# One written-out instruction order, two moves: a block of scores ahead of two transposes, and one weight load behind a softmax product

## The chip, the cores and the metric

The kernel runs on one core of a Trainium2 chip (trn2). A core has five engines with instruction queues of their own: TensorE (PE in the profile, its weight loads PEld), VectorE (DVE), ScalarE (ACT), GpSimd (POOL) and SyncE (SP), and 16 DMA engines that they share. Each queue runs in order. The metric is the time of one execution on the device in microseconds, as a median of several runs. A profiled execution gives, beside its own time, a trace of every instruction, every DMA packet and the TensorE clock that was granted.

## What the kernel computes

A causal attention with a window of 64 positions, whose output goes straight into a two-layer block with a cosine gate:

```python
scores = q @ k.transpose(0, 1, 3, 2) / np.sqrt(D)     # q, k, v: 8 batches, 8 heads, 576 positions, 64
rel = pos[:, None] - pos[None, :]
scores = np.where((rel >= 0) & (rel < 64), scores, -1e9)
scores = scores - np.max(scores, axis=-1, keepdims=True)
attn = np.exp(scores)
attn = attn / (np.sum(attn, axis=-1, keepdims=True) + 1e-09)
x = (attn @ v).transpose(0, 2, 1, 3).reshape(4608, 512)
h = x @ w_in                                          # w_in: 512 x 2048
out = (h * np.cos(h)) @ w_out                         # w_out: 2048 x 512
```

Inputs and output are float32; the matmuls take bf16.

## The kernel before

**Tiling.** The 4608 rows of x are cut into nine token tiles of 512. For each, TensorE multiplies by w_in (the columns of 128 give 16 results, h), ScalarE makes the sine with a phase of pi/2, VectorE multiplies h by it, and TensorE multiplies by w_out. The attention of a later batch is worked into the matmuls of an earlier tile. Only the beginning has nothing to hide behind: tile 0 needs the attention of batch 0 first, and that is what this case is about.

**The order at the beginning** is written out by hand in the string `FIRST` (lines 52 to 71). A loop (line 724) splits it into steps and calls one function for each; since every engine's queue is in order, the order of the string is the order on each engine. A later planner (`at`, `pump`, lines 615 to 622) orders the rest and isn't touched. The steps that matter here, with the pair of heads as first number and, for scores, a half of the query blocks (0 or 1) as the second:

- `Lq0`, `Lk0`, `Lq1`, `Lk1`, `Lv0`: loads of q, k (L169) and v (L192), issued from GpSimd, which casts on the way. (The first pair of batch 0, `Lq0.0` and `Lk0.0`, comes through SyncE instead, L174.) `Lwi.i` loads a quarter of w_in (L208), `Lwo.i` a quarter of w_out (L211). Each is an instruction on GpSimd's queue of 0.6 to 0.9 us.
- `tq`, `tk` (batch 0) and `Tq`, `Tk` (batch 1): twelve transposes on TensorE of one pair of heads into PSUM (L225), in a ring of three buffers. `pq`, `pk`, `Pq`, `Pk` copy the result to SBUF, on VectorE (`.d`) or ScalarE (`.a`) (L130, L259, L261).
- `s.p.g.bank`: the scores of one group of batch 0, that is four blocks of 64 queries of a pair of heads, into a PSUM bank (L358 puts the mask into the bank with two matmuls, L365 adds eight score matmuls). `Gs` is the same for batch 1.
- `m`: the negative maximum of a group (VectorE, L375). `e`: the exponentials and their sums (ScalarE, L392). `i`: the reciprocal of the sums (VectorE, L402). `n.p.g.p`: the product of the two, `w`, on GpSimd (L409). `w.p.g`: four transposes of it on TensorE (L425). `c`: its copy to SBUF (VectorE, L130).
- `zA`, `zB`, `zC`: copies of half a v block to other partitions. `v.a.g`: the products with v (L462), `x.a.g`: their copy to xT (ScalarE or VectorE, L130).
- `h.g.f.bank`: a half of tile 0 times two column blocks of w_in (L476), eight matmuls. `h.0.0` and `h.0.1` read the first piece of w_in, `h.0.2` and `h.0.3` the second, `h.0.4` and `h.0.5` the third, `h.0.6` and `h.0.7` the fourth.

`s.p.g` frees nothing until its exponentials are done: the five banks are shared by the groups, and a bank can be written again after `e` has read it (for `s.3.0` the bank of group `0.0`, for `s.2.1` that of group `0.1`).

In the span of the change the order on TensorE is `s.2.0`, `Tq.0`, `Tk.0`, `s.3.0`, `Tq.1`, `Tk.1`, `s.2.1`, `Gs.10`, `Gs.9`, `w.0.0`, `w.1.0`, `Gs.12`, `w.2.0`, `w.3.0`, `v.0.0`, and on GpSimd `Lv0.3`, `Lwi.0`, `Lwi.1`, `Lwi.2`, `n.1.0`, `n.0.0`, `n.2.0`, `n.3.0`, `n.0.1`, `n.1.1`, `n.2.1`, `Lwi.3`. Four transposes of a constant (L423) stand in front of those of `w.3.0`.

Of the kernel before, what the change touches and what calls it, by code (L numbers as in the profile page):

```python
# [10 lines left out]
def _safe_warn(msg, *a, **kw):  # L11
# [40 lines left out]
FIRST = (  # L52
    "io Lq0.0 Lk0.0 mk cq.d mc ck.a tq.0 fa.1 Lq0.1 pq.0.d Lk0.1 tk.0 fb.1 pk.0.a s.0.0.0 Lq0.2 tq.1 fc.1 tk.1 m.0.0 "
    "pq.1.a s.0.1.1 Lk0.2 tq.2 pk.1.d s.1.0.2 Lq0.3 Lk0.3 tk.2 s.1.1.3 e.0.0 tq.3 m.0.1 Lq1.0 Lk1.0 Lq1.1 pq.2.d "
    "pk.2.d Lk1.1 tk.3 m.1.0 s.2.0.4 Lv0.0 Lv0.1 Tq.0 Lv0.2 pk.3.d m.2.0 e.0.1 pq.3.a i.0.0 e.1.0 Tk.0 s.3.0.0 Tq.1 "
    "e.2.0 Lv0.3 Lwi.0 Pq.0.d i.1.0 Lwi.1 m.3.0 m.1.1 i.2.0 Pk.0.a e.3.0 Lwi.2 Tk.1 n.1.0.p s.2.1.1 Pq.1.d Gs.10.2 "
    "m.2.1 Gs.9.4 n.0.0.p Pk.1.a n.2.0.p i.3.0 e.1.1 w.0.0 zA.0.d w.1.0 c.0.0.d Gs.12.0 w.2.0 n.3.0.p i.0.1 c.1.0.d "
    "zA.1.d c.2.0.d e.2.1 zB.0.s zB.1.s n.0.1.p i.1.1 w.3.0 v.0.0 c.3.0.d x.0.0.a s.3.1.3 Gm.10 v.1.0 m.3.1 i.2.1 "
    "Gs.11.2 Gm.9 Gm.12 n.1.1.p x.1.0.a e.3.1 w.0.1 w.1.1 c.1.1.a i.3.1 h.0.0.1 h.0.1.4 tb n.2.1.p c.0.1.d Lwi.3 "
# [744 lines left out]
```

## Time and profile before

| what | us |
|---|---|
| time, median of three runs | 296.46 |
| the three runs | 296.46, 296.06, 297.11 |
| the profiled execution's own time | 297.33 |
| its span, first to last instruction | 295.5 |
| what lies around the span (297.33 less 295.5) | 1.8 |
| TensorE busy in the span | 288.2 |
| mean granted TensorE clock (1 is full) | 0.994 |

The span is what the engines' rows add up to, with times counted from its start. A row of the timeline has the start, the duration (of several merged instructions their total stretch), the engine, the line, the operation, what it writes and reads, and, in brackets, how long the engine was idle before it and what ended that. The chain of work that ended last has the start, the duration, the engine and the line. A row of the windows has, for a stretch of time, the busy time of each engine, the granted clock, the share of the DMA engines' time and GB/s; a DMA share above 1 means that packets overlapped in an engine. In a row of DMA issues the last number is the time from issue to landing.

### The profile page before, as it was taken

The page shows a single profiled execution, that of the slowest core. Times are in us where ns is not written, and L with a number is a line of the kernel's source. Part 1 is how long each engine was busy: PE and PEld are TensorE (multiplying, and loading weights), DVE is VectorE, ACT ScalarE, POOL GpSimd, SP SyncE. Part 2 cuts the span into 40 slices and gives each one's busy share as a digit, 9 for nine tenths or more (in the row PEclk, how much of TensorE's full clock was granted, in tenths as well). Part 3 has the DMA queues.
Part 4 walks back from the last instruction along what each step waited for, and adds up shares of the span by engine and source line. Part 5 has one row for each costly group of instructions (what it writes and reads, how often), then busy time and mean ns, then how long its engine had stood idle before and what let it go on. Part 6 is the DMA issues. An engine that isn't in the chain of part 4 may idle for free.

```text
span 295.5 us, 8290 instructions
## 1 busy us (share of the span) xinstructions
PE 288.2 (98%) x2815; PEld 163.4 (55%) x2815; DVE 231.0 (78%) x906; ACT 237.9 (80%) x791; POOL 209.9 (71%) x230
## 2 busy tenths in 40 slices
PE   8879999999999999999999999999999999999995
PEld 3658864544454444444454445444547854884495
DVE  3987888888797876788668876996689868957863
ACT  5989699887988799869986999699967896937710
POOL 9899749993699849995999399948995476033200
PEclk9989999999999999999999999999999999999999
DMA  7999999999999999999999999999959315042013
GB/s 145 177 198 190 186 196 137 151 129 153 151 265 128 151 235 172 114 182 215 174 166 150 225 172 152 155 213 179 146 129 194 41 38 177 2 114 86 0 38 107
DMA packets 168267, 43.81 MB, mean 148 GB/s; under 512 B 155616, under 2 KB 163872, under 8 KB 168224
## 3 DMA queue, kind: packets, MB, share of 16 engines
q0 software_dynamic: 100896, 18.06, 82.3%
q1 hardware_dynamic: 67184, 25.15, 47.0%
q8 instruction: 22, 0.36, 0.5%
q14 instruction: 21, 0.17, 0.2%
q10 hardware_dynamic: 144, 0.07, 0.1%
HBM read 36.70 MB, written 9.44 MB: 156 GB/s over the span
## 4 chain that ended last, share of the span: by engine, by line
PE 93%; POOL 3%; DVE 2%; issue 0%; ACT 0%; POOLq 0%
PE h_ps L512 37%; PE out_ps L764 24%; PE out_ps L601 13%; PE h_ps L476 5%; PE o_ps L444 3%; PE out_ps L495 3%; PE s_ps L327 3%; POOL w L409 2%; PE busy L137 2%; PE tw_ps L425 1%; DVE negm L375 1%; DVE kT L130 1%; PE o_ps L462 1%; PE s_ps L365 1%; POOL v L130 0%; PE tk_ps L225 0%
## 5 line engine op out<-in xcount | busy, mean ns | idle before, releaser
L512 PE MATMUL h_ps<-xT,w_in 128*128 128x512 bf16 x512 | 111.8, 379 | 0.0
L409 POOL TENSOR_TENSOR w<-e,rden 128x512 bf16<-128x512 f32 (+1 forms) x68 | 69.4, 1033 | 48.8 <-DVE rden L402 38.1
L751 DVE TENSOR_TENSOR gT<-h_ps,sin 128x512 bf16<-128x512 f32 x128 | 84.6, 687 | 21.8 <-ACT sin L748 20.4
L392 ACT ACTIVATE e<-s,negm 128x128 f32<-128x128 f32 (+1 forms) x256 | 97.2, 382 | 2.6 <-DVE negm L380 1.6
L748 ACT ACTIVATE sin<-h_ps 128x512 f32<-128x512 f32 x128 | 73.5, 599 | 25.3 <-PE h_ps L512 23.5
L512 PEld LDWEIGHTS <-w_in 128*128 128x128 bf16 x512 | 50.2, 98 | 59.3
L764 PE MATMUL out_ps<-w_out,gT 128*128 128x512 bf16 x320 | 72.0, 379 | 0.0
L380 DVE CUSTOM_DVE_ANT_0 s<-s_ps,mask 128x128 f32<-128x128 f32 (+1 forms) x256 | 55.7, 276 | 0.3 <-PE s_ps L327 0.3
L764 PEld LDWEIGHTS <-gT 128*128 128x128 bf16 x320 | 30.4, 98 | 35.5
L392 ACT ACTIVATION_READ_ACCUMULATOR e<-s,negm 128x1 f32 x256 | 48.1, 188 | 0.0
L192 POOL DMA_DIRECT2D v<-in_v_dram x40 | 34.0, 869 | 0.7 <-DMA q<-in_q_dram 0.5
L186 POOL DMA_DIRECT2D q<-in_q_dram x30 | 26.2, 892 | 3.3 <-PE tq_ps L225 3.0
L186 POOL DMA_DIRECT2D k<-in_k_dram x30 | 26.2, 884 | 0.0
L402 DVE RECIPROCAL rden<-den 128x4 f32<-128x4 f32 (+1 forms) x73 | 12.0, 166 | 18.0 <-ACT e L392 17.8
L130 POOL COPY v<-v 64x1536 bf16<-64x1536 bf16 (+3 forms) x16 | 22.9, 1431 | 0.4
L380 DVE DVE_READ_ACCUMULATOR2_ANT negm<- 128x1 f32 x256 | 21.2, 83 | 0.0
L541 POOL TENSOR_TENSOR qT<-gT 128x512 bf16<-128x512 bf16 x12 | 13.6, 1156 | 9.1 <-DVE gT L751 9.0
L130 DVE CAST xT<-o_ps 128x512 bf16<-128x512 f32 x24 | 15.5, 681 | 5.1 <-PE o_ps L444 4.5
L601 PEld LDWEIGHTS <-gT 128*128 128x128 bf16 x152 | 13.9, 98 | 2.2
L495 PE MATMUL out_ps<-w_out,gT 128*128 128x512 bf16 x64 | 14.7, 380 | 0.0
L476 PE MATMUL h_ps<-xT,w_in 128*128 128x256 bf16 x128 | 14.6, 273 | 0.0
L572 DVE TENSOR_TENSOR out_sb<-out_ps,p 128x512 f32<-128x512 f32 (+2 forms) x16 | 8.6, 548 | 6.7 <-ACT p L130 5.6
(92 smaller groups left out, 327.9 us busy)
## 6 DMA issues: line engine op xcount, KB each, us to landing
out_dram<-out_sb SPq DMA_DIRECT2D x16, 512.0 KB, 8.4
v<-in_v_dram POOLq DMA_DIRECT2D x32, 128.0 KB, 5.9
q<-in_q_dram POOLq DMA_DIRECT2D x24, 128.0 KB, 8.6
k<-in_k_dram POOLq DMA_DIRECT2D x24, 128.0 KB, 6.5
w_in<-in_moe_w_in_dram POOLq DMA_DIRECT2D x4, 512.0 KB, 9.2
w_out<-in_moe_w_out_dram POOLq DMA_DIRECT2D x4, 512.0 KB, 10.9
q<-in_q_dram POOLq DMA_DIRECT2D x7, 144.0 KB, 6.2
k<-in_k_dram POOLq DMA_DIRECT2D x7, 144.0 KB, 6.3
```

The lines of the kernel that those rows point to most:

```text
L130: {"a": nc.scalar.copy, "p": nc.gpsimd.tensor_copy}.get(engine, nc.vector.tensor_copy)(out, in_)
L186: nc.gpsimd.dma_start(out=st[name, b][0:n, c].rearrange("p (h d) -> p h d", h=H), in_=src.rearrange("h p d -> p h d"))
L192: nc.gpsimd.dma_start(out=vt.rearrange("p (h d) -> p h d", h=H), in_=v[b, :, c * 128:c * 128 + n, :].rearrange("h p d -> p h d"))
L380: nc.vector.tensor_tensor_reduce(out=s[:, u, c], in0=s_ps[:, u, c], in1=mask[:, 2 - j % 2 if j else 0, c], scale=-scale if b else -1.0, sc ...
L392: nc.scalar.activation(e[:, u, c], s[:, u, c], AF.Exp, bias=negm[:, u:u + 1], scale=1.0 if n < n_first else -1.0, accum_out=den[:, u:u + 1])
L409: (nc.gpsimd if engine == "p" else nc.vector).tensor_tensor(out=w[:, 0:u], in0=e[:, 0:u], op=ALU.mult, in1=rden[:, 0:u].unsqueeze(2).to_br ...
L476: nc.tensor.matmul(out=h_ps[:, half * e:half * e + half], lhsT=w_in_sb[:, ks, ff * 128:ff * 128 + 128], rhs=st["xT", 0][:, ks, half * g:ha ...
L512: nc.tensor.matmul(out=st["h", ff], lhsT=w_in_sb[:, ks, ff * 128:ff * 128 + 128], rhs=st["xT", mt][:, ks], start=start, stop=stop)
L601: nc.tensor.matmul(out=to[n_] if split else to[:, e], lhsT=lhs[name][f // 2][:, f % 2, 128 * e:128 * e + 128], rhs=rhs[name][:, f, lo:hi], ...
L748: nc.scalar.activation(sin, h_ps, AF.Sin, bias=math.pi / 2.0)
L751: nc.vector.tensor_tensor(out=gt[:, e], in0=h_ps, in1=sin, op=ALU.mult)
L764: nc.tensor.matmul(out=o_ps[e], lhsT=gT[ff // 2][:, ff % 2, ms * 128:ms * 128 + 128], rhs=w_out_sb[:, ff], start=ff == 0, stop=ff == n_ff - 1)
```

## The change

Two moves in `FIRST`, and nothing else:

- TensorE: `s.3.0` goes ahead of `Tk.0`, and `s.2.1`, which stood behind `Tk.1`, goes with it. The order is then `s.2.0`, `Tq.0`, `s.3.0`, `s.2.1`, `Tk.0`, `Tq.1`, `Tk.1`, `Gs.10`. The banks stay as they were.
- GpSimd: `Lwi.2` goes from ahead of `n.1.0` to behind it. The order is then `Lwi.1`, `n.1.0`, `Lwi.2`, `n.0.0`.

No instruction is added or removed, and the orders on VectorE and ScalarE are the same as before.

```diff
-    "pk.2.d Lk1.1 tk.3 m.1.0 s.2.0.4 Lv0.0 Lv0.1 Tq.0 Lv0.2 pk.3.d m.2.0 e.0.1 pq.3.a i.0.0 e.1.0 Tk.0 s.3.0.0 Tq.1 "
-    "e.2.0 Lv0.3 Lwi.0 Pq.0.d i.1.0 Lwi.1 m.3.0 m.1.1 i.2.0 Pk.0.a e.3.0 Lwi.2 Tk.1 n.1.0.p s.2.1.1 Pq.1.d Gs.10.2 "
+    "pk.2.d Lk1.1 tk.3 m.1.0 s.2.0.4 Lv0.0 Lv0.1 Tq.0 Lv0.2 pk.3.d m.2.0 e.0.1 pq.3.a i.0.0 e.1.0 s.3.0.0 s.2.1.1 "
+    "Tk.0 Tq.1 e.2.0 Lv0.3 Lwi.0 Pq.0.d i.1.0 Lwi.1 m.3.0 m.1.1 i.2.0 Pk.0.a e.3.0 Tk.1 n.1.0.p Lwi.2 Pq.1.d Gs.10.2 "
```

## The prediction, made before the changed kernel was run

> **What bounds the kernel now.** I read the page first, then the chain of waits in order of time, then the timelines of the engines over the stretch that the change touches, and last the landings of the loads.
>
> ```profile
> PE 93%; POOL 3%; DVE 2%; issue 0%; ACT 0%; POOLq 0%
> ```
>
> The chain that ended last is TensorE for 93% of the span. A change outside it must move the place where TensorE takes over. The chain in order of time shows that place:
>
> ```profile
> 13.27 0.64 DVE qT L130
> 13.91 0.08 DVE rden L402
> 13.99 0.59 DVE negm L375
> 14.65 0.74 POOL w_in L208
> 15.39 0.07 issue
> 15.45 4.10 POOL w L409 x4
> 19.60 0.56 PE tw_ps L425 x4
> 20.15 0.57 PE o_ps L462 x8
> ...
> 28.07 10.59 PE h_ps L476 x96
> ```
>
> From 14.65 to 19.60 GpSimd carries the chain: the issue of w_in's third piece, then four products w (`n.1.0`, `n.0.0`, `n.2.0`, `n.3.0`). At 19.60 TensorE gets the last of them (`w.3.0`) and from there the chain is its own work, but for a few later pieces on other engines that wait on that work in turn. So what makes the fourth product ready earlier moves the rest with it, as far as nothing else stands in the way.
>
> **The load behind the product.** GpSimd's timeline:
>
> ```profile
> 10.67 1.75 POOL L192 DMA_DIRECT2D v<-in_v_dram  x2 [0.47 <-DMA q<-in_q_dram]
> 12.40 1.51 POOL L208 DMA_DIRECT2D w_in<-in_moe_w_in_dram  x2
> 14.64 0.74 POOL L208 DMA_DIRECT2D w_in<-in_moe_w_in_dram  x1 [0.73 <-DVE negm L375]
> 15.45 6.13 POOL L409 TENSOR_TENSOR w<-e,rden 128x512 bf16<-128x512 f32 x6
> ```
>
> GpSimd is idle for 0.73 us (13.91 to 14.64), then issues for 0.74, and the first product starts at 15.45. That product needs its exponentials and one reciprocal, and the chain has the end of that reciprocal at 13.91 + 0.08 = 13.99. After the change it can start there. What does the issue wait for? The profile names VectorE's maximum, which a load into w_in does not use. A row above has another GpSimd load waiting for the landing of a q load: counted in the written order, the thirteenth load from GpSimd waits for the fifth, eight back. The third piece of w_in is the seventeenth, so its ninth is q of batch 1's pair 1:
>
> ```profile
> 6.92 0.68 POOL L169 DMA_DIRECT2D q<-in_q_dram  x1
> ```
>
> ```profile
> q<-in_q_dram POOLq DMA_DIRECT2D x1, 144.0 KB, 7.4
> ```
>
> ```profile
> 14.40 0.45 PE L225 MATMUL tq_ps<-ident,q 96*64 96x96 bf16 x12 [0.76 <-DMA q<-in_q_dram]
> ```
>
> That q landed about 7.4 us after its issue at 6.92, at 14.3, and TensorE's transposes of it began at 14.40 at its landing. I take this landing for the wait. Behind the product the issue comes at 15.0, when it is long past.
>
> The sum from 13.99: before, to the end of the fourth product, 15.45 + 4.10 = 19.55. After: one product (4.10 / 4 = 1.025) to 15.02, the issue (0.74) to 15.76, the gap (0.07), three products (3.08) to 18.91. Gain 0.64; its bounds are 0.58 with another such gap and 0.73, the whole idle time.
>
> The second and third products need reciprocals that are older than their turn, and the fourth one that comes at 16.83:
>
> ```profile
> 15.17 0.72 DVE L130 COPY qT<-tq_ps 128x576 bf16<-128x576 bf16 x1
> 15.81 0.68 DVE L375 TENSOR_REDUCE negm<-s_ps 128x4 f32<-128x512 f32 x1
> 16.83 0.18 DVE L402 RECIPROCAL rden<-den 128x4 f32<-128x4 f32 x1 [0.34 <-ACT e L392]
> 17.98 0.42 DVE L130 COPY wT<-tw_ps 128x512 bf16<-128x512 bf16 x1 [0.34 <-PE tw_ps L425]
> 18.83 0.85 DVE L130 COPY v<-v 64x512 bf16<-64x512 bf16 x1
> ```
>
> It ends at 17.01; the product's turn is 17.88. The copy of the first transposed w waits 0.34 for TensorE at 17.98, and with the second product 0.64 earlier that wait is gone; VectorE is then late next: its copy of v ends at 19.68 - 0.34 = 19.34, and TensorE wants it for `v.0.0` at 20.15 - 0.64 = 19.51. Cover 0.17.
>
> What the moved issue pushes: behind it stand only products, all earlier than before. The piece itself is issued at 15.02 instead of 14.64, 0.38 later. Its landing:
>
> ```profile
> w_in<-in_moe_w_in_dram POOLq DMA_DIRECT2D x1, 512.0 KB, 8.2
> w_in<-in_moe_w_in_dram POOLq DMA_DIRECT2D x1, 512.0 KB, 11.9
> w_in<-in_moe_w_in_dram POOLq DMA_DIRECT2D x1, 512.0 KB, 5.7
> ```
>
> ```profile
> 23.59 0.80 POOL L208 DMA_DIRECT2D w_in<-in_moe_w_in_dram  x1
> ```
>
> ```profile
> 28.00 3.23 PE L476 MATMUL h_ps<-xT,w_in 128*128 128x256 bf16 x28
> ```
>
> The landings are those of the first, third and fourth pieces, then stand the issue of the fourth and the matmuls that read the third and fourth. The third needs 11.9 us from issue to landing (14.64 + 11.9 = 26.5), the first 8.2 (12.40 + 8.2 = 20.6): 5.9 us between the two landings where the issues are 2.2 apart, so the third queues behind older loads and an issue 0.38 later should change its landing by nothing; the bound is 0.38. Its reader is `h.0.4` at 28.00, 27.36 after the gain: cover 0.4 to 0.8.
>
> [...] The two issues from 12.40 took 1.51, 0.76 each, with a bf16 copy beside them (13.27 in the chain), against 0.74 beside maxima; by the rows it is 0.02.
>
> **The scores ahead of the transposes.** TensorE's timeline, and ScalarE's copy of `Tk.0`:
>
> ```profile
> 13.04 0.40 PE L358 MATMUL s_ps<-mask,ident 64*64 64x512 bf16 x2
> 13.28 0.36 PE L365 MATMUL s_ps<-kT,qT 64*64 64x64 bf16 x8
> 14.70 0.45 PE L225 MATMUL tk_ps<-ident,k 96*64 96x96 bf16 x12
> 15.08 0.40 PE L358 MATMUL s_ps<-mask,ident 64*64 64x512 bf16 x2
> 15.32 0.75 PE L365 MATMUL s_ps<-kT,qT 64*64 64x128 bf16 x22
> 17.55 0.62 PE L425 MATMUL tw_ps<-ident,w 128*128 128x128 bf16 x8 [1.48 <-POOL w L409]
> ```
>
> ```profile
> 14.71 0.69 ACT L130 COPY kT<-tk_ps 128x576 bf16<-128x576 bf16 x1
> ```
>
> `s.2.1` (two mask matmuls, eight scores, 15.08 to about 15.5) moves into the hole of 0.76 that ends at 14.40. `s.3.0` moves from 13.04 to about 12.6. `Tk.0` then begins near 13.4 and ends near 13.8; ScalarE copies it at 14.71, so 0.9 us of cover. `Tq.1` stays at its landing, 14.40, and `Tk.1` at 14.70. Nobody takes the earlier scores up earlier: VectorE works without a pause until the maxima of `s.3.0` (13.99) and `s.2.1` (15.81). `Gs.10` needs ScalarE's copy that ends at 15.40. So this half is worth nothing on the path, and its loss is bounded by the cover. If `Tk.0` came over 0.9 us late, ScalarE would stall with all exponentials behind it.
>
> **The clock.** Three stretches of 3.41 us, each with its length, the busy times of PE, PEld, DVE, ACT and POOL, the granted clock, the DMA share and GB/s:
>
> ```profile
> 12.86:16.27 3.41, 2.45 (x70) 1.79 (x64) 3.41 (x9) 3.41 (x20) 2.62 (x4) 1.00 2.29 158
> 16.27:19.69 3.42, 1.77 (x25) 1.25 (x26) 2.71 (x7) 3.42 (x20) 3.42 (x5) 1.00 1.31 205
> 19.69:23.10 3.41, 3.41 (x58) 2.49 (x58) 2.89 (x18) 1.81 (x7) 2.39 (x3) 0.50 1.23 220
> ```
>
> After a stretch with 52% busy TensorE (1.77 of 3.42) the granted clock is 0.50 for the next, after one with 72% it stays 1.00. The half clock falls where TensorE has taken over, so it can cost up to 3.41 / 2 = 1.7 us. With the w chain 0.64 earlier, 1.77 becomes some 2.4 of 3.42 (70%), near the stretch that kept the clock. What would then be late is the third piece: landing 26.5, reader at 28.00, so at most 1.5 of gain in all. For the fourth (23.59 + 5.7 = 29.3, read 24 matmuls after 28.00 at 10.59 / 96 each, 30.65) the limit is 1.35, unless its earlier issue brings it forward.
>
> [...]
>
> **The sum.** Profiled execution, 297.33: 0.64 gives 296.7 with the half clock kept, the limit of 1.35 to 1.5 gives 295.8 to 296.0 without. But it is 0.87 above the median of 296.46 and above all three runs. The three lie 1.05 apart, about what half a clock costs after the landings have cut it, so I read the low one, 296.06, as an execution that does not pay it, and has little left to gain before the landings bind. The median run then gains something between 0.2 and 0.8. I take the chain's 0.64, trimmed to 0.6: 295.9, own range 295.5 to 296.4. About 0.3% (0.9 us) is what a measurement of this kernel can tell from no change, so this is inside it.
>
> **The rivals.**
>
> 1. The clock and the chain both pay in the median run. For it: 70% against the 72% that kept the clock. Against: the landings. 296.46 less 1.35 to 1.5 gives 295.0 to 295.1; faster by over 0.3%.
> 2. The 0.73 of idle time belongs to GpSimd and not to the load: whatever ended with VectorE's maximum holds the product too. It then starts at 14.65, the issue follows at 15.67, and the fourth product ends at 19.55 as before. For it: the profile names that maximum. Against: the landing at 14.3 and the 13th load's wait. Or the landings hide all. 296.3 to 296.5.
> 3. Slower: the early stretch is emptied. `s.2.1` leaves 15.08, and with the holes after 13.8 a stretch that begins at 13.6 holds 14.40 to 15.1 and a few scores, some 1.2 of 3.41 us, a third. The clock is then halved from 17.0, and what lies there (17.55 to 19.60) takes twice as long; if TensorE also fails to win it back for the next stretch, the whole takeover runs at half clock: 296.46 + 1.35 = 297.8. It decides when two halved stretches follow one another. Against: the stretch at 0.50 was busy throughout and the clock came back after it; with one halved stretch the gain of 0.64 is lost and little more.
>
> **How the numbers follow.** Forecast 0.55, first rival 0.23, second 0.15, third 0.07. Faster by over 0.3% (below 295.57): the first rival and a little of the forecast's range, 0.30. Slower: 0.07. Same: 0.63. The predicted time is 295.9. The range runs from the first rival's 295.0 to 296.8, the second's upper end and the spread of the runs above it.
>
> **What would show it.** Right: the first product on GpSimd at 14.0, the issue of w_in at 15.0 with no wait before it, the fourth product's end near 18.9, `w.3.0` near 18.95, `Tk.0` near 13.4 with ScalarE's copy still at 14.71, and the third piece landing at 26.5. The clock rows tell the first and third rivals: no 0.50 stretch between 19 and 23, or one that begins near 17. Wrong: a first product at 14.6; `h.0.4` or `h.0.6` waiting for w_in; ScalarE idle before 14.71; a span below 294 or above 296.5.

## The result, and the profile after

The change made the kernel 0.6% slower.

| | before | after |
|---|---|---|
| time, median of 19 runs each, us | 296.98 | 298.86 |
| lowest and highest, us | 295.55, 299.17 | 297.36, 300.56 |
| ratio after to before, 95% interval | | 1.0062 [1.0044, 1.0081] |
| the profiled execution's own time, us | 297.33 | 298.86 |
| its span, us | 295.5 | 297.1 |
| its mean granted TensorE clock | 0.994 | 0.989 |

The chain that ended last, by engine, after. TensorE's share was 93% before:

```profile
PE 89%; POOL 3%; DMA 2%; DVE 2%; issue 1%; ACT 1%; POOLq 0%
```

The same chain in order of time (start, duration, engine, line). GpSimd, which carried it from 14.65 to 19.60 before, does not occur in this stretch:

```profile
15.41 1.42 ACT e L392 x8
16.83 0.02 issue
16.86 0.18 DVE rden L402
17.04 2.29 DVE v L130
19.33 0.33 DVE wT L130
...
20.08 0.94 DVE v L130
21.02 0.04 issue
21.06 0.53 PE o_ps L462 x12
```

TensorE takes over at 21.06 instead of 19.60. One row stands out: VectorE spends 2.29 us of the chain on a copy of v, `zA.0`, which was no part of it before. GpSimd's timeline after shows that GpSimd itself did what was predicted:

```profile
14.31 1.04 POOL L409 TENSOR_TENSOR w<-e,rden 128x512 bf16<-128x512 f32 x1
15.30 0.81 POOL L208 DMA_DIRECT2D w_in<-in_moe_w_in_dram  x1
16.12 3.05 POOL L409 TENSOR_TENSOR w<-e,rden 128x512 bf16<-128x512 f32 x3
19.82 1.04 POOL L409 TENSOR_TENSOR w<-e,rden 128x512 bf16<-128x512 f32 x1 [0.65 <-DVE rden L402]
```

The issue stands behind the first product, waits for nothing, and the fourth product ends at 16.12 + 3.05 = 19.17 (before 19.55). Now VectorE's timeline after:

```profile
16.95 2.37 DVE L130 COPY v<-v 64x512 bf16<-64x512 bf16 x1
19.25 0.41 DVE L130 COPY wT<-tw_ps 128x512 bf16<-128x512 bf16 x1
19.67 0.38 DVE L130 COPY wT<-tw_ps 128x512 bf16<-128x512 bf16 x1
20.08 0.93 DVE L130 COPY v<-v 64x512 bf16<-64x512 bf16 x1
```

The copy of 64x512 began at 16.95, as before (16.93), but lasted 2.37 us instead of 0.72. (The same copy lasts 0.29 us in e6 below, so its row holds its wait; where such a row starts is called below where the copy "asks".) It ended at 19.32, 0.16 behind the end of the third of the three products (19.17). The copies of the transposed w behind it came at 19.25 and 19.67 instead of 17.98 and 18.41. TensorE's timeline after shows who waited for them:

```profile
17.24 0.62 PE L425 MATMUL tw_ps<-ident,w 128*128 128x128 bf16 x8 [1.22 <-POOL w L409]
19.71 0.59 PE L423 MATMUL tw_ps<-ident 128*128 128x128 bf16 x4 [0.55 <-DVE wT L130]
20.09 0.63 PE L425 MATMUL tw_ps<-ident,w 128*128 128x128 bf16 x4
24.43 2.04 PE L476 MATMUL h_ps<-xT,w_in 128*128 128x256 bf16 x16
29.22 1.49 PE L476 MATMUL h_ps<-xT,w_in 128*128 128x256 bf16 x12
```

The first transposes of w come earlier (17.24 for 17.55), so the load's move did what it was for. Then the ring of three transposed tiles is full until VectorE empties one: `w.3.0` starts at 20.09 instead of 19.60, `h.0.0` at 24.43 instead of 23.34, `h.0.4` at 29.22 instead of 28.00. Of the 1.6 us by which the span grew, 1.2 are there by then. The row of `h.0.0` before:

```profile
23.34 1.91 PE L476 MATMUL h_ps<-xT,w_in 128*128 128x256 bf16 x16
```

The stretches of the granted clock after (length, busy PE, PEld, DVE, ACT and POOL, clock, DMA share, GB/s):

```profile
14.45:17.86 3.41, 1.73 (x41) 1.31 (x35) 3.20 (x7) 3.41 (x17) 3.40 (x4) 1.00 1.89 181
17.86:21.27 3.41, 2.77 (x31) 1.87 (x32) 3.35 (x6) 2.31 (x14) 2.35 (x3) 0.50 1.23 207
21.27:24.68 3.41, 3.41 (x56) 2.63 (x53) 3.36 (x24) 2.07 (x8) 2.24 (x3) 0.50 1.19 235
```

Two stretches in a row are halved, where before had one. The third piece's landing (issues of w_in, the last number is the time from issue to landing) is not to blame: 15.30 + 11.4 = 26.7, where before had 26.5, and that is 2.5 ahead of `h.0.4`.

```profile
w_in<-in_moe_w_in_dram POOLq DMA_DIRECT2D x1, 512.0 KB, 11.4
```

### The profile page after: what moved, and what is told of

It is laid out like the page before. It is cut to its first block, busy times and chain, and to the rows that moved or that the text cites. A ratio compares the mean times of both kernels' runs of the same rounds, so it can differ in the third digit from the quotient of the medians.

```text
span 297.1 us, 8262 instructions
## 1 busy us (share of the span) xinstructions
PE 286.9 (97%) x2787; PEld 164.4 (55%) x2815; DVE 232.8 (78%) x906; ACT 239.1 (80%) x791; POOL 210.2 (71%) x230
## 4 chain that ended last, share of the span: by engine, by line
PE 89%; POOL 3%; DMA 2%; DVE 2%; issue 1%; ACT 1%; POOLq 0%
PE h_ps L512 37%; PE out_ps L764 23%; PE out_ps L601 13%; PE h_ps L476 5%; PE o_ps L444 3%; PE out_ps L495 3%; PE s_ps L327 3%; DMA k<-in_k_dram 2%; DVE v L130 1%; POOL w L409 1%; ACT e L392 1%; PE tw_ps L425 1%; POOL q L169 1%; PE o_ps L462 1%; POOL v L130 0%
## 5 line engine op out<-in xcount | busy, mean ns | idle before, releaser
L764 PE MATMUL out_ps<-w_out,gT 128*128 128x512 bf16 x305 | 68.7, 379 | 1.1 <-issue 0.8
L392 ACT ACTIVATION_READ_ACCUMULATOR e<-s,negm 128x1 f32 x256 | 48.8, 191 | 0.0
L541 POOL TENSOR_TENSOR qT<-gT 128x512 bf16<-128x512 bf16 x12 | 13.6, 1153 | 9.1 <-DVE gT L751 9.0
L495 PE MATMUL out_ps<-w_out,gT 128*128 128x512 bf16 x61 | 14.3, 380 | 0.3 <-issue 0.2
```

Of the source, the lines that this page charges most:

```text
L392: nc.scalar.activation(e[:, u, c], s[:, u, c], AF.Exp, bias=negm[:, u:u + 1], scale=1.0 if n < n_first else -1.0, accum_out=den[:, u:u + 1])
L764: nc.tensor.matmul(out=o_ps[e], lhsT=gT[ff // 2][:, ff % 2, ms * 128:ms * 128 + 128], rhs=w_out_sb[:, ff], start=ff == 0, stop=ff == n_ff - 1)
```

## The experiments

Two theories stood after the result. A, the copy: VectorE's copy of v cannot run while GpSimd's products run back to back, and everything behind it on VectorE is late. B, the clock: TensorE has less to do, above all by the scores' move, and loses its clock for 6.8 us. Every kernel ran beside runs of before on the same chip, and the ratios are to those (their medians: 296.99 us beside e1 to e4, 296.75 beside e5 to e8, 296.69 beside e9 to e12, 296.85 beside e13 to e15).

### The two halves of the change, and the copy in another form

`e1_load_only` is before with the load's move alone (here and below, the diffs show the pieces of `FIRST` that differ):

```diff
-e.3.0 Lwi.2 Tk.1 n.1.0.p s.2.1.1
+e.3.0 Tk.1 n.1.0.p Lwi.2 s.2.1.1
```

`e2_scores_only` is before with the scores' move alone:

```diff
-e.1.0 Tk.0 s.3.0.0 Tq.1
+e.1.0 s.3.0.0 s.2.1.1 Tk.0 Tq.1
...
-n.1.0.p s.2.1.1 Pq.1.d
+n.1.0.p Pq.1.d
```

> Only the load's move: w_in's third piece behind the first product, TensorE's order as before. Theory A (the copy): the GpSimd products now stand so that VectorE's first copy of v is held until the last of them ends; that copy takes 2.0 to 2.5 us as in the changed kernel instead of 0.72, and the time is 1.3 to 2 us above before (298.3 to 299 where before has 297). Theory B (the clock): the emptier TensorE after the scores' move halves the clock for 6.8 us instead of 3.4; here the scores stay late, so a half clock of 3.4 us at most and a time of 296.3 to 297.2. If both moves matter alike, something near 298.

> Only the scores' move on TensorE, the load ahead of the first product as before. Theory A: the copy takes 0.7 to 0.9 us as before, and the time is that of before within 0.3 us. Theory B: a half clock of 6.8 us and 1.3 to 2 us above before.

Measured: e1 298.96 us, 1.0064 [1.0029, 1.0099]; e2 296.85 us, 0.9992 [0.9970, 1.0015]. The load's move is the whole loss, the scores' move is nothing. The copy in VectorE's timeline of e1:

```profile
17.00 2.24 DVE L130 COPY v<-v 64x512 bf16<-64x512 bf16 x1
```

And of e2, where it lasted 0.61 us beside a row of six products:

```profile
16.28 0.61 DVE L130 COPY v<-v 64x512 bf16<-64x512 bf16 x1
```

The clock goes with the load as well: the profiled execution of e1 has a mean clock of 0.989 without the scores' move, as after has with its two halved stretches, that of e2 0.994 with it, as before has with its one; and all seven runs of e1 have a mean clock of 0.994 or less, eight of the twelve of e2 one of 0.999 or more. So B's cause, the scores, is out; that the clock carries part of the loss is not.

`e3_after_reduce_copy` (after) and `e4_before_reduce_copy` (before) make `zA.0` and `zA.1` as maxima over an axis of length one, which give the same values:

```diff
+            if b == 0 and hi == 1:
+                nc.vector.tensor_reduce(out=to[:, 0], in_=of[:, 0].unsqueeze(2), op=ALU.max, axis=AX.X)
+            else:
-            copy(engine, to, of)
+                copy(engine, to, of)
```

> [...] Theory A (it is the copy that waits for GpSimd's products): each takes about 0.65 us whatever GpSimd does, the first transposed w is copied at 17.7 instead of 19.25, w.3.0 starts at 19.0 instead of 20.1, and the time is 295.8 to 296.8, at or below before. Theory B: the half clock of 6.8 us stays and the time stays within 0.4 us of the changed kernel's, 298.5 to 299.

> The kernel before with the same two copies made as reductions. Theory A: before pays little for the wait (its copies took 0.72 and 0.85 beside products, and the first ended before VectorE was needed), so the time is that of before or up to 0.5 us below, and its spread from run to run shrinks if the copies' luck makes the spread. Theory B: no change.

Measured: e3 297.30 us, 1.0013 [0.9992, 1.0035]; e4 296.72 us, 0.9995 [0.9974, 1.0015]. In VectorE's timeline of e3 the first lasts 0.65 us beside the same row of products:

```profile
16.57 0.65 DVE L206 TENSOR_REDUCE v<-v 64x512 bf16<-64x512 bf16 x1
```

Most of the loss is gone with nothing changed but the form of two copies, though the time stays above the 295.8 to 296.8 that A expected. B expected no change. So the copy is the cause: beside the same row of products it took 2.37 us in after, and the reduction that writes the same values 0.65 in e3. Why the one form waits and the other does not, no profile shows.

With the copy out of the way w_in becomes the bound, as TensorE's timeline of e3 shows:

```profile
24.15 1.05 PE L479 MATMUL h_ps<-xT,w_in 128*128 128x256 bf16 x8 [0.76 <-DMA w_in<-in_moe_w_in_dram]
27.39 3.77 PE L479 MATMUL h_ps<-xT,w_in 128*128 128x256 bf16 x33 [0.47 <-DMA w_in<-in_moe_w_in_dram]
```

### When does the copy get in?

The copy does not simply wait for the product that runs when it asks: after's copy let two ends of products pass (at about 17.2 and 18.2) and got in at the third, while before's, asked for at 16.93, was done 0.15 behind the very next end (17.49). The first guess was that it has to ask early enough ahead of an end (0.56 us in before, 0.23 in after).

`e5_copy_ahead` lets it ask earlier in after:

```diff
-n.2.0.p i.3.0 e.1.1 w.0.0 zA.0.d w.1.0
+n.2.0.p zA.0.d i.3.0 e.1.1 w.0.0 w.1.0
```

`e6_before_copy_late` lets it ask later in before:

```diff
-w.0.0 zA.0.d w.1.0 c.0.0.d
+w.0.0 w.1.0 c.0.0.d zA.0.d
```

`e7_pause` puts the issue of after where the copy asks, so that GpSimd has no product there:

```diff
-n.1.0.p Lwi.2 Pq.1.d Gs.10.2 m.2.1 Gs.9.4 n.0.0.p Pk.1.a
+n.1.0.p Pq.1.d Gs.10.2 m.2.1 Gs.9.4 n.0.0.p Lwi.2 Pk.1.a
```

> The kernel after with one swap on VectorE: the first copy of v (zA.0.d) stands ahead of the reciprocal i.3.0 instead of behind it, so it asks some 0.3 us earlier. Theory A (the copy of v is shut out by GpSimd's products, and gets in at a product's end only when it asked about half a microsecond ahead of it, as in the kernel before with 0.56): it starts at about 16.6, some 0.5 us ahead of the product's end at 17.2, is done by 17.4 (0.75 us long instead of 2.37), w.3.0 starts by 19.3 and the time is 296.6 to 297.3, ratio 0.998 to 1.001. If it is shut out at that end all the same, the fourth product has to wait for the reciprocal behind the copy, the products pause at about 18.2, and the copy ends at about 18.35. Theory B (TensorE has too little to do and loses its clock, whatever the copy does): the 6.8 us of half clock stay and the time is 298.5 or more.

> The kernel before, with only the first copy of v moved one place down on VectorE, behind the eviction c.0.0, so that it asks at about 18.35, some 0.15 us ahead of a product's end (18.51), with more products in a row behind it. No load and no scores are moved. Theory A: it is shut out at that end and after it, until the row of products pauses; the sixth product's reciprocal stands behind the copy, so that is after the fifth, at about 20.6: the copy lasts 2 us or more, w.3.0 starts a microsecond later than the 19.60 of before, and the time is 298 to 299.5, ratio 1.004 to 1.010. Rival (a copy waits for one product at most): it ends at 18.7, w.3.0 is not later than 19.7 and the time stays at 296.7 to 297.3. Theory B expects the same as the rival: TensorE's work is unchanged.

> The kernel after with the third piece's issue one product further down, between GpSimd's products n.0.0 and n.2.0, so that GpSimd does 0.8 us of issuing, and no product, at about 16.4 to 17.2, when the copy of v asks (16.95). Theory A: the copy finds no product in its way and lasts 0.65 to 0.8 us, w.3.0 starts when the fourth product has ended, at about 19.3, and the time is 296.6 to 297.4, ratio 0.998 to 1.001. Theory B: TensorE's work ahead of 17.9 is the same, so the half clock stays at 6.8 us and the time at 298.5 or more. The third piece, issued 1.1 us later than in after, should still land at 26.4 to 26.8.

Measured: e5 298.06 us (with one run of 303.59, which the ratio leaves out), 1.0047 [1.0023, 1.0071]; e6 297.14 us, 1.0012 [0.9991, 1.0034]; e7 299.53 us, 1.0084 [1.0057, 1.0112]. A's first expectation failed in all three. In e5 the copy asked 0.6 us ahead of the end at 17.09 and was not let in:

```profile
16.48 1.76 DVE L130 COPY v<-v 64x512 bf16<-64x512 bf16 x1
```

It ended at 18.24, 0.16 behind the start of a pause of GpSimd, whose next product waited for the reciprocal behind the copy; that was the case held in reserve. (The profiled execution of e5, 296.19 us, was the fastest of its twelve and does not stand for its median.) In e6 the copy asked only 0.14 us ahead of an end and got in at once:

```profile
18.29 0.29 DVE L130 COPY v<-v 64x512 bf16<-64x512 bf16 x1
```

In e7 it asked during the issue (16.03 to 16.84) and stayed out over that and two products:

```profile
16.03 0.81 POOL L208 DMA_DIRECT2D w_in<-in_moe_w_in_dram  x1
16.85 2.06 POOL L409 TENSOR_TENSOR w<-e,rden 128x512 bf16<-128x512 f32 x2
```

```profile
16.73 2.33 DVE L130 COPY v<-v 64x512 bf16<-64x512 bf16 x1
```

The time of e7 is one that B expected, but its profiled execution took 298.62 at full clock, so the clock alone does not make it.

So the lead does not decide. What the cases share is the place of the issue. Where the copy stayed out, its row of products had begun some 10 ns behind an issue that itself stood behind a product (after: 15.30 + 0.81 = 16.11, then 16.12). Where it got in, the row had begun 0.07 us behind an issue (before, the row "issue" at 15.39 of the chain), and in the trace its first product carries a wait on GpSimd's own semaphore, which `n.0.0` in after, the first of its row, does not.

### The issue's place

`e10_after_again` is after once more. `e11_load_behind_row` puts the third piece's issue in after behind the fourth product:

```diff
-n.1.0.p Lwi.2 Pq.1.d
+n.1.0.p Pq.1.d
...
-w.2.0 n.3.0.p i.0.1
+w.2.0 n.3.0.p Lwi.2 i.0.1
```

`e12_load_behind_row_alone` does the same in before:

```diff
-e.3.0 Lwi.2 Tk.1 n.1.0.p
+e.3.0 Tk.1 n.1.0.p
...
-w.2.0 n.3.0.p i.0.1
+w.2.0 n.3.0.p Lwi.2 i.0.1
```

> The kernel after once more, unchanged, for a second profile and a second set of times. Theory A: the copy of v is shut out again past two products' ends, 2.2 to 2.5 us; the time is 298 to 299.5, ratio 1.003 to 1.009. If the copy's 2.37 us had been an accident of one execution, it is 0.6 to 0.9 here and in most runs, and the time must come from elsewhere.

> The kernel after with the third piece's issue three products further down, behind n.3.0, so that no issue of a DMA stands between GpSimd's four products. What is to be told apart is what shuts the copy out. In every profile so far in which it passed a product's end and stayed out (after, e1, e5, e7, e8), the row of products had started 10 ns behind an issue, itself directly behind a product; where it got in at the next end (before, e2, e6), the row had started 65 ns behind an issue. If that is it: here the copy gets in at the next end, and lasts 0.5 to 1.1 us; the first product at about 14.2 is 1.2 us earlier than in before and the four end at 18.4, so w.3.0 starts at about 18.9 instead of 19.60, and the time is 295.9 to 296.8, ratio 0.997 to 1.000. If rows of products shut the copy out wherever the issue is, it ends behind the fourth product or a pause, at 18.5 or later, and the time is 298 or more. The third piece, issued at about 18.4, should land at 26.5 to 27, since its data wait for the second's (23.5).

> The kernel before with the third piece's issue behind n.3.0, as in e11, and the scores and transposes left where before has them. The scores' move alone was worth nothing (e2), so both theories give it the time of e11 within 0.5 us: 295.9 to 297.0 if the copy gets in at a product's end, 298 or more if it is shut out.

Measured: e10 298.91 us, 1.0068 [1.0043, 1.0093], the copy 2.23 us; e11 296.84 us, 0.9997 [0.9977, 1.0017], the copy 0.69; e12 297.11 us, 1.0010 [0.9989, 1.0031]. e12 holds both cases in one trace. GpSimd, then VectorE's two copies:

```profile
14.54 4.09 POOL L409 TENSOR_TENSOR w<-e,rden 128x512 bf16<-128x512 f32 x4
18.58 0.81 POOL L208 DMA_DIRECT2D w_in<-in_moe_w_in_dram  x1
19.40 1.05 POOL L409 TENSOR_TENSOR w<-e,rden 128x512 bf16<-128x512 f32 x1
```

```profile
17.43 0.30 DVE L130 COPY v<-v 64x512 bf16<-64x512 bf16 x1
18.73 1.88 DVE L130 COPY v<-v 64x512 bf16<-64x512 bf16 x1
```

The first asked within the undisturbed row and got in at the next end (17.58). The second asked during the issue and stayed out over it and the product behind it, until 20.45. (The profiled execution of e12, 298.68, was the slowest of its twelve; whether the second copy stays out in the others too is not known.)

In e11 neither copy of v asked behind the issue. GpSimd, then VectorE's two copies:

```profile
14.85 4.09 POOL L409 TENSOR_TENSOR w<-e,rden 128x512 bf16<-128x512 f32 x4
18.89 0.81 POOL L208 DMA_DIRECT2D w_in<-in_moe_w_in_dram  x1
```

```profile
17.35 0.69 DVE L130 COPY v<-v 64x512 bf16<-64x512 bf16 x1
18.80 0.29 DVE L130 COPY v<-v 64x512 bf16<-64x512 bf16 x1
```

The second asked 0.09 ahead of the issue, got in at the fourth product's end (18.94) and was done while the issue ran. So in this one case the issue did not keep out a copy that had asked before it.

e11 has the gain that the prediction was after, and shows that it is worth nothing measurable. TensorE's timeline of e11:

```profile
19.00 0.40 PE L425 MATMUL tw_ps<-ident,w 128*128 128x128 bf16 x4 [0.19 <-POOL w L409]
22.05 1.91 PE L476 MATMUL h_ps<-xT,w_in 128*128 128x256 bf16 x16
27.31 2.79 PE L476 MATMUL h_ps<-xT,w_in 128*128 128x256 bf16 x24 [0.20 <-DMA w_in<-in_moe_w_in_dram]
30.34 0.83 PE L476 MATMUL h_ps<-xT,w_in 128*128 128x256 bf16 x6 [0.24 <-DMA w_in<-in_moe_w_in_dram]
```

`w.3.0` starts 0.60 earlier than in before and `h.0.0` 1.29 earlier, of which some 0.7 is the half clock that before had between the two (3.74 us from one to the other, 3.05 in e11). But `h.0.4` waits for the third piece and is 0.69 earlier, and `h.0.6` waits for the fourth and is 0.29 earlier than the 30.63 of before. All twelve runs of e11 had the full clock, and their 296.84 is not below the 296.63 of before's runs at full clock.

`e13_drain` keeps the change and lets GpSimd wait for itself behind the issue, by two tiny instructions (the step `dr`) of which the second reads what the first writes:

```diff
-n.1.0.p Lwi.2 Pq.1.d
+n.1.0.p Lwi.2 dr Pq.1.d
...
+        nc.gpsimd.memset(tiny, 0.0)
+        nc.gpsimd.tensor_tensor(out=tiny, in0=tiny, in1=tiny, op=ALU.mult)
```

`e14_before_issue_in_row` makes the loss without the change: before, with the fourth piece's issue drawn into the row:

```diff
-m.2.1 Gs.9.4 n.0.0.p
+m.2.1 Gs.9.4 Lwi.3 n.0.0.p
...
-n.2.1.p c.0.1.d Lwi.3
+n.2.1.p c.0.1.d
```

`e15_tiny_no_wait` is the control to e13; its two tiny instructions have nothing to do with each other, so that it tells GpSimd's wait apart from any short instruction behind the issue:

```diff
-        nc.gpsimd.tensor_tensor(out=tiny, in0=tiny, in1=tiny, op=ALU.mult)
+        nc.gpsimd.memset(tiny2, 0.0)
```

> The kernel after with two tiny instructions of GpSimd (a memset of 128x8 and a product of it with itself, which waits on GpSimd's own semaphore until the memset is done) between the third piece's issue and the second product n.0.0. Nothing reads the result. Theory A1 (a row that starts 10 ns behind an issue keeps VectorE's copy out, a row that starts after GpSimd has waited for itself, as in before, 65 ns behind the issue, does not): the copy gets in at the first product's end that follows, at about 17.4, and lasts 0.6 to 0.9 us; the row starts 0.2 us later than in after, w.3.0 starts at 19.0 to 19.5, and the time is 296.0 to 297.2, ratio 0.997 to 1.001. Theory A2 (any issue within the row does it): the copy lasts 2 us or more and the time is 298 or more.

> The kernel before, with its third piece, scores and transposes where they were, and the fourth piece's issue drawn forward into the row of products, directly behind the first one (n.1.0). A1 and A2: the copy of v is shut out from the issue on, over n.0.0, n.2.0 and n.3.0, until the row pauses at about 20.3: it lasts 3 us or more, and the time is 299 to 301, ratio 1.008 to 1.014. Of this 0.8 us is the row's own delay by the issue, so a copy that gets in at 18.3 (under 1.6 us long) with a time of 297 to 298 would speak against the issue as the cause, and leave only the third piece's own move.

> The control to e13_drain: two tiny memsets to two tiles in the same place, with no wait between them. [...]

Measured: e13 297.38 us, 1.0028 [1.0005, 1.0052]; e14 300.46 us, 1.0114 [1.0084, 1.0144]; e15 299.37 us, 1.0077 [1.0051, 1.0103]. GpSimd and the copy in e14:

```profile
16.73 0.81 POOL L208 DMA_DIRECT2D w_in<-in_moe_w_in_dram  x1
17.55 3.04 POOL L409 TENSOR_TENSOR w<-e,rden 128x512 bf16<-128x512 f32 x3
```

```profile
17.11 3.64 DVE L130 COPY v<-v 64x512 bf16<-64x512 bf16 x1
```

It stayed out from the issue to 0.16 behind the third product's end. In e13 the wait is the gap between the two tiny instructions, 16.23 to 16.32, and the copy gets in at the next product's end (17.51):

```profile
15.31 0.81 POOL L208 DMA_DIRECT2D w_in<-in_moe_w_in_dram  x1
16.10 0.13 POOL L704 MEMSET tiny<- 128x8 f32 x1
16.32 0.20 POOL L705 TENSOR_TENSOR tiny<-tiny 128x8 f32<-128x8 f32 x1
16.49 4.13 POOL L409 TENSOR_TENSOR w<-e,rden 128x512 bf16<-128x512 f32 x4
```

```profile
17.11 0.56 DVE L130 COPY v<-v 64x512 bf16<-64x512 bf16 x1
```

In e15, with two tiny memsets and no wait, the copy took 2.30 us:

```profile
16.87 2.30 DVE L130 COPY v<-v 64x512 bf16<-64x512 bf16 x1
```

This settles when the copy is kept out in this kernel. Where GpSimd went from a product through an issue straight on to more products, the copy of v that asked from the issue on stayed out until GpSimd paused (2.37 us in after, 2.30 in e15, 3.64 in e14), and a wait of GpSimd on itself behind the issue ended that (0.56 in e13). (The second tiny instruction is a product in e13 and a memset in e15, so the two kernels differ in that as well; but in after products stand directly behind the issue and let nothing in.) e13's time lies a little above the range expected for it: the wait costs the row 0.36 us, so that its fourth product ends at 19.56, as in before.

### How the late copy costs time

`e8_after_filled` and `e9_before_filled` fill TensorE where it is idle, with work that nobody reads: 16 transposes of the identity ahead of `w.0.0`, and a step `fk` of three 128x512 matmuls into a free bank ahead of `w.3.0`:

```diff
-            for i in range(GF if n == FILL[0] else 0):
-                nc.tensor.transpose(t_ps[:, i], ident, ident)
+            for i in range({FILL[0]: GF, 0: 4 * GF}.get(n, 0)):
+                nc.tensor.transpose(t_ps[:, i % GF], ident, ident)
...
-i.1.1 w.3.0 v.0.0
+i.1.1 fk.3 w.3.0 v.0.0
```

> The kernel after with work that nobody reads added on TensorE where it stands idle: 16 transposes of the identity ahead of w.0.0 and three 128x512 matmuls ahead of w.3.0, 1.5 us in all. VectorE and GpSimd are as in after, so the copy of v should still last 2.2 to 2.4 us. It tells how the late copy costs time. If by the clock alone (an idle TensorE is put to half speed): no half clock, and the time is that of the runs of before at full clock, 296.3 to 296.8. If by its own lateness alone (w.3.0 at 20.1 instead of 19.6, the first matmuls of the halves 1.1 us later): the time stays at 297.9 or more though the clock is full. Between them, both have a share.

> The control to e8_after_filled: the kernel before with the same unread work on TensorE (16 transposes of the identity ahead of w.0.0, three 128x512 matmuls ahead of w.3.0). The clock should be full. If the filling itself is free, the time is that of the runs of before at full clock, 296.0 to 296.8, and the 3 us between it and e8 (299.65) belong to the load's move, without any half clock: theory A (the copy of v shut out by the products). If the filling costs by itself, this kernel is slow as well, 298.5 to 299.8, and e8 tells nothing of the clock.

Measured: e8 299.65 us, 1.0101 [1.0062, 1.0140]; e9 298.76 us, 1.0067 [1.0038, 1.0095]. The filling costs by itself, so neither tells anything against the kernels without it. But against each other they do: in the runs without a halved stretch e8 took 299.62 us (median of 5) and e9 298.31 (of 7), so the change costs some 1.3 us at full clock. That is a rough figure: these few runs lie up to 1.5 and 2.5 us apart, and the two ran on different chips (with runs of before at 296.75 and 296.69 beside them).

The unfilled runs say the same. The mean granted clock of each run tells how many stretches were halved in it (3.41 / 2 of 297 us is 0.006 each):

| halved stretches | before, runs and median us | after, runs and median us |
|---|---|---|
| none | 77, 296.63 | 2, 297.51 |
| one | 28, 297.15 | 8, 298.21 |
| two | 2, 298.48 | 16, 299.45 |
| three | none | 1, 300.00 |

With equal clock, after is 0.9 to 1.1 us longer; and it has most often two halved stretches where before has most often none, at 0.5 to 1.3 us each. So, as an estimate from these rows, about half of the loss is the late copy itself, and about half the clock; three entries rest on one or two runs. That the clock is lost because TensorE waits for the late copy is shown only in part. With the copy free, e3 and e13 had more than one halved stretch in 1 of their 24 runs (after in 17 of 27). But they still had at least one in 16 of 24, against 30 of 107 in before, so part of the clock's loss seems to come with the change by another way than the copy.

## Why the prediction was wrong

- **GpSimd's steps were right, about 0.3 us later than predicted.** First product 14.31 (predicted 14.0), issue 15.30 with no wait (15.0), fourth product's end 19.17 (18.91). The second rival, that the idle time belongs to GpSimd, is out.
- **The step that failed:** "VectorE is then late next: its copy of v ends at 19.68 - 0.34 = 19.34, and TensorE wants it for `v.0.0` at 20.15 - 0.64 = 19.51. Cover 0.17." The term that was mis-sized is VectorE's copy of v: both copies were counted at the durations that before's trace had, 0.72 and 0.85. Those already held a wait for GpSimd: before's first copy ended 0.15 behind a product's end, and e6's, which asked 0.14 ahead of an end, lasted 0.29 in all. Moving the issue into the row turned this short wait into 2.37 us. The second copy then ended at 21.01 instead of 19.34, and `w.3.0` came at 20.09 instead of 18.95.
- **What the copy and GpSimd do to each other was weighed in one direction only.** The prediction asked what a copy on VectorE does to GpSimd's issue and put that at 0.02 us. The issue did take 0.81 instead of 0.74, which is still little. It did not ask what GpSimd does to VectorE's copy, which took 2.37 us instead of 0.72, and that was the loss.
- **The scores' move** was worth nothing, as predicted (e2). `Tk.0` ran at 13.75 (predicted 13.4) and ScalarE's copy at 14.77 (14.71).
- **The third piece's landing** was right: 26.7 for 26.5.
- **The clock** went the other way: TensorE was busy for 1.73 us of the stretch ahead, where 2.4 was expected, and two halved stretches followed. That is what the third rival described, but not its cause: it blamed the scores, and e1's profiled execution has the clock of two stretches (0.989) without them. The rival's stretch from 13.6 was a supposition; the halved ones began at 17.86 in after and at 19.69 in before. The half clock that the first rival hoped to win back was missing from most runs of before: 77 of 107 had none.
- **The gain was overrated as well.** e11 has `w.3.0` 0.60 us earlier and a free copy, and its time is that of before: `h.0.4` and `h.0.6` waited for landings. The limit of 1.35 took the fourth piece to land at 29.3, 5.7 us behind its issue; in e11 it was issued 0.90 earlier and took 7.6, to 30.3.
- **The range started too low.** It was worked out from a median of three runs, 296.46. Over 19 runs the kernel before takes 296.98, above the range's upper end of 296.8 even with no change.

## What to carry to other kernels

Before an instruction is moved on GpSimd, look at the VectorE copies beside it. Here the copies of v, from SBUF to SBUF, ended some 0.15 us behind the end of a GpSimd product, and their recorded duration was no constant: 0.29 to 3.64 us for the same 64x512. So a copy that ends like that may have waited. In this kernel a DMA issue between two GpSimd products cost more than its 0.8 us (1.9 us in after, 3.6 in e14) because such a copy asked behind it; ahead of the row (before), behind it (e11, e12) or with the copy in another form (e3) the loss was gone or small. And work out the next bound (here the landings) before crediting a gain on the chain.

## What the runs showed of the hardware that was not expected

- GpSimd kept VectorE's copy out over several instructions: 2.23 to 2.37 us in after, e1, e7, e10 and e15, 3.64 in e14, 1.76 in e5 and 1.88 in e12, always ending some 0.16 us behind the last product ahead of a pause. In a row that did not start directly behind such an issue, the copies got in at the next end and lasted 0.29 to 0.86 us (before, e2, e6, e11, e13, and the first of e12). In e13, where GpSimd waits for its own work to end, the copy took 0.56 us; why that wait lets it in, no profile shows.
- Unread work on an idle TensorE made before slower by 1.7 us at full clock (298.31 in e9 against 296.63). In the profile of e9 (an execution of 300.50 with one halved stretch) TensorE waited 2.0 us for transposing DMAs at 117 to 119 us, in that of e8 2.2 us in all. Why they came late stays open.
